# A recurrent attention and a three-way maxout layer on one core: another order for every engine's work and for both load queues

## Chip, core and metric

The kernel runs on 1 core of one Trainium2 chip. The metric is the device time of one launch, in microseconds (us), as the median of several runs. The engines that it uses are TensorE (PE: matrix products, with PEld for its weight loads), VectorE (DVE), ScalarE (ACT), GpSimd (POOL) and SyncE (SP, which only issues DMAs here).

## What is computed

```python
for t in range(S):                       # B, H, S, D = 4, 8, 768, 48
    state = alpha[:, :, t, :, None] * state + einsum('bhd,bhe->bhde', k[:, :, t], v[:, :, t])
    y[:, :, t] = einsum('bhd,bhde->bhe', q[:, :, t], state)
x = y.transpose(0, 2, 1, 3).reshape(B * S, H * D)      # 3072 x 384
h = maximum(maximum(x @ w1, x @ w2), x @ w3)           # 3072 x 768
out = h @ w_out                                        # 3072 x 384
```

Inputs and output are float32; q, k, v and alpha are 4 x 8 x 768 x 48, the weights 384 x 768 (three) and 768 x 384.

## The kernel before

The recurrence is done in chunks. There are 12 steps; step s is a window of 256 tokens of batch s % 4 (window s // 4), and has two units of 128 tokens (U = 2). A token row pair is folded into one partition (R = 2), so that a tile holds 128 partitions of 8 heads, 2 tokens and 48 numbers.

For each step the decays are logarithms that a triangular product sums (c, `sums`), and their exponentials scale q and k (`decay_in`, `decay_out`, `totals`, `scale_k`, `scale_q`). q and k are turned by PE (T and t) in steps 0 to 4 and by a transposing DMA (D) in steps 5 to 11. The scores (A) are masked on DVE (a), and the outputs are the chunk's own part and the state's part (Y, `attend`). The state is updated (S, s), decayed (M, z) and spread (y). Then x is kept in float16 (x), and the layer follows: nine gate pieces G per step, of six products each, with their maxima (h), and the output pieces O with a scaling and a store (o).

What runs when is written out by hand. `ORDER` is a string of some 800 pieces. A piece is a letter, a number, an optional engine (v, p or a for DVE, POOL or ACT) and `@step`. `emit` calls one function per piece, and every engine executes its pieces in the order of the string; waits between engines are put in by the framework (`tc.manual_schedule`). So the string is also the order of the two load queues:

- `l0`, `l1`, `l2`, `l3` load alpha, k, q and v of a step (384 KB each); without a letter they are issued by SP, with `a` by ACT, between ACT's own computing pieces. Each input has a ring of four tiles (`NQ`), so a load of step s waits for the readers of step s - 4.
- `K0` to `K8` load parts of w1, w2, w3 (`K` number i: weight i % 3, columns i // 3), `K9` to `K11` parts of w_out, into eight staging tiles; `W` casts the part to float16. `G`'s number is 3 x (pair of column tiles) + weight, so `G0` needs `W0`, `G1` needs `W1`, and so on.
- Stores (`o`) and transposing DMAs (`D`) are issued by SP, in the same queue as its loads.
- `H` is an idle product: `warm` multiplies a zero tile, 128 x 512, as often as its number says, and nothing reads the result.

All results of PE go to one pool of eight banks (`bank`); a new one waits until the last reader of the bank's previous content is done. An idle product takes a bank too, once per call.

```python
    queues = {"": nc.sync, "a": nc.scalar}
    def warm(_, n, *x):
        wps = bank([P, 512], "wps")
        for _ in range(n):
            nc.tensor.matmul(wps, blank[:, :P], blank, start=True, stop=True)
```

Of the kernel before, what the change touches and what calls it, by code (L numbers as in the profile page):

```python
# [23 lines left out]
def kernel(  # L24
# [422 lines left out]
    def emit(order):  # L447
# [20 lines left out]
        W7p@0 r0@5 G7@2 h7v@2 T0@3 q1p@3 T1@3 G7@1 z0p@3 K8@0 e0@4 w0p@4 f0@4 l3@4 s1v@3 v0a@3
        t1v@3 t0a@3 k1v@4 G6@0 h6a@1 q1p@4 h7v@1 l2@6 u0p@4 c0@5 A0@3 a0@3 A1@3 T1@4 q0p@4 a2@3
        W8a@0 G8@2 a3@3 h8v@2 G8@0 g0@5 h6a@0 a1@3 f0@5 G8@1 k0p@4 T0@4 e0@5 h8v@1 G7@0 v1p@3  # L470
        Y0@3 Y2@3 t1a@4 V0a@4 t0a@4 h7v@0 y0p@3 Y3@3 x0a@3 x1a@3 K11@0 l1@5 K9a@0 v1p@4 S0@4
        W11a@0 A0@4 s0v@4 K10a@0 a1@4 A1@4 a3@4 M0p@4 z0p@4 s1v@4 u0p@5 G0@3 l0@6 a0@4 G7@3
        l1a@6 a2@4 v0v@4 y0a@4 m0p@6 r0@6 G3@3 h3a@3 G1@3 G6@3 Y0@4 r1@5 l3a@5 h0v@3 Y3@4 h8v@0
        Y2@4 x1v@4 N0@6 Y1@4 x0a@4 W9a@0 l2@5 G8@3 M1v@1 c0@6 e0@6 f0@6 G0@4 h1v@3 k0v@5 q1v@5
        G3@4 w0v@5 q0v@5 M0p@5 W10a@0 g0@6 u0v@6 r1@6 G1@4 l0@7 m0v@7 G2@4 k1p@5 D1@5 h0a@4
        z1p@1 k0p@6 O0@1 h1v@4 w0v@6 D0@5 q0p@6 D0@6 k1p@6 q1p@6 O1@1 N0@7 l0@8 h6a@3 l3@6 h2v@4
        l2@7 l1a@7 o1a@1 h7v@3 D1@6 h3v@4 o0a@1 V0a@5 O0@2 o0a@2 O1@2 y1p@1 G7@4 h8v@3 S0@5 A0@5
# [6 lines left out]
        a0@6 Y2@6 Y0@6 O1@0 x1v@6 o0a@0 l0@10 r1@8 l3a@8 x0v@6 G4@6 G3@6 V0a@7 v1a@7 G0@6 h5v@5
        M1v@4 z1p@4 G8@5 h2v@5 h3a@6 h7v@5 h4v@6 S0@7 h0a@6 v0p@7 l3@11 o1a@0 h8v@5 y1a@4 A0@7
        a1@7 s0v@7 u0p@8 A1@7 a2@7 m0p@9 a3@7 M0p@7 z0p@7 y0p@7 k0p@8 Y1@7 a0@7 r0@9 l1a@9 G2@6
        G1@6 h1v@6 q1p@8 G6@6 h6v@6 s1v@7 G5@6 Y0@7 Y2@7 N0@9 l2@9 m0v@10 w0v@8 q0p@8 D0@8 Y3@7
        k1v@8 D1@8 x0a@7 x1a@7 l3@9 G8@6 G7@6 r1@9 G6@7 h6a@7 G0@7 V0v@8 c0@9 e0@9 O1@3 g0@9
        M1p@5 u0v@9 k0v@9 O0@3 f0@9 w0p@9 G4@7 q1p@9 k1p@9 D1@9 q0p@9 D0@9 o1a@3 o0a@3 V0a@11
        h2v@6 h5v@6 h7v@6 h8v@6 G8@7 G7@7 h7v@7 h0a@7 S0@8 N0@10 s0v@8 O0@5 o0a@5 A0@8 a0@8 A1@8  # L490
        a2@8 l0@11 Y1@8 G3@7 v1a@8 h3a@7 l1a@10 O1@5 c0@10 a3@8 z0p@8 y0p@8 Y3@8 o1a@5 a1@8 Y2@8
        e0@10 h8v@7 g0@10 v0p@8 Y0@8 G1@7 x0a@8 f0@10 V0a@9 v0p@9 x1v@8 G1@8 h4v@7 l2@10 M1v@6
        z1v@6 z1v@5 y1a@5 l3@10 G0@8 h1v@7 M0p@9 h0a@8 S0@9 A1@9 A0@9 s0v@9 z0p@9 y0p@9 G6@8
        l1@11 G2@8 a0@9 v1p@9 G2@7 G5@7 h6a@8 r0@10 r1@10 M0p@10 u0p@10 Y3@9 a3@9 a1@9 a2@9
        m0v@11 l2a@11 q1p@10 k1v@10 D1@10 Y0@9 Y1@9 x0a@9 Y2@9 G7@8 h2v@7 h1v@8 x1a@9 r0@11 G4@8
        G8@8 G6@9 G3@9 w0p@10 N0@11 c0@11 f0@11 h5v@7 e0@11 h6v@9 V0v@10 q0v@10 k0p@10 D0@10
        O0@4 O1@4 g0@11 v0a@10 h7v@8 h2v@8 G4@9 h8v@8 G5@8 O1@7 r1@11 v1p@10 S0@10 h3a@9 h4v@9
        o0a@4 o1a@4 q1p@11 k1v@11 o1a@7 M1p@7 D1@11 s0v@10 A0@10 a0@10 A1@10 a3@10 u0p@11 k0p@11
        G7@9 z0p@10 y0a@10 y1p@6 G8@9 G3@8 h3a@8 O0@7 a1@10 w0v@11 a2@10 h7v@9 h8v@9 Y3@10 Y1@10
        Y0@10 Y2@10 G1@9 G0@9 x1v@10 x0a@10 G4@10 z1p@7 q0p@11 D0@11 h4v@8 h0a@9 h5v@8 h1v@9  # L500
        G2@9 G3@10 o0a@7 v1p@11 h2v@9 S0@11 s0v@11 A0@11 A1@11 a0@11 a3@11 h3a@10 G6@10 G0@10
# [42 lines left out]
```

## Time and profile before

| | |
|---|---|
| median of 3 runs | 150.43 us (149.96 to 150.75) |
| profiled execution: span from first to last instruction | 147.1 us |
| the median less the span (launch and end, outside the span) | 3.3 us |
| PE / DVE / ACT / POOL busy | 137.7 / 120.5 / 100.7 / 89.7 us |
| idle products (L435) | 35, 9.7 us busy |
| loads and stores | 32.43 MB, 220 GB/s over the span |
| DMA issues of loads: SP / ACT | 50 / 10 |

The page's first part gives each engine's busy time. The second cuts the span into 40 slices of 3.7 us, with a busy digit for each. The chain of waits goes back from the last instruction to what released it. A timeline row reads: start, duration, engine, line, operation, output and inputs by the program's names, how many were merged, and in brackets the idle time before and what ended it. `SPq` and `ACTq` are the issuing of DMAs by an engine's sequencer. Names: `ra rk rq rv` are the loaded inputs, `ws` a staged weight, `wcat` a cast one, `lps` the sums, `aps` scores, `yps` outputs, `gps` gate products, `ops` output products, `wps` idle products, `ob` what is stored.

### The profile page before, as it was taken

Reading aid. Unit: us, or ns where it says so; the run is one execution under the profiler, and the core shown is the slowest. Engines: PE = TensorE matmul, PEld = TensorE weight load, DVE = VectorE, ACT = ScalarE, POOL = GpSimd, SP = SyncE. Lnnn points to the kernel's source line nnn. Section 1 sums busy time; section 2 is a strip of 40 time slices with the busy share of each in tenths; the row PEclk is TensorE's granted clock in tenths of the full one; section 3 lists DMA queues with packets and bytes.
Section 4 is the critical chain, followed back from the end, with each engine's and each line's share of the span. In section 5 each row is a group of like instructions: output and inputs, shape, how many; then the busy total and the mean of one; then the engine's idle time right before and its main releaser. Section 6 shows DMA issues by size and latency. Waiting matters only on the chain.

```text
span 147.1 us, 5524 instructions
## 1 busy us (share of the span) xinstructions
PE 137.7 (94%) x2301; PEld 105.4 (72%) x2301; DVE 120.5 (82%) x224; ACT 100.7 (68%) x207; POOL 89.7 (61%) x147
## 2 busy tenths in 40 slices
PE   6996888999999999999999999999899999999990
...
ACT  3669998878999978958699467795375463213170
...
DMA  5999999999999978999999979999987880021163
GB/s 114 321 325 341 326 312 282 322 288 334 328 298 241 286 225 155 202 289 187 303 156 325 327 218 155 237 269 276 288 117 222 91 113 0 4 75 37 53 241 134
DMA packets 73032, 32.43 MB, mean 220 GB/s; under 512 B 65456, under 2 KB 73008, under 8 KB 73008
## 3 DMA queue, kind: packets, MB, share of 16 engines
...
## 4 chain that ended last, share of the span: by engine, by line
PE 38%; DMA 18%; POOL 16%; ACT 9%; SPq 8%; issue 4%; DVE 4%; POOLq 0%; DVEq 0%; ACTq 0%
PE gps L388 21%; DMA rv<-in_v_dram 11%; PE ops L421 10%; SPq L96 7%; POOL qk L231 6%; DMA ws<-in_moe_w_dram 5%; PE yps L306 3%; DMA qkT<-qk 3%; POOL kept L372 2%; POOL ka L198 2%; PE aps L286 2%; POOL st L151 2%; ACT vu L149 1%; POOL wcat L151 1%; POOL vu L151 1%
## 5 line engine op out<-in xcount | busy, mean ns | idle before, releaser
L388 PE MATMUL gps<-xT,wcat 128*128 128x256 f16 x648 | 76.5, 273 | 1.5 <-DVE hT L405 0.6
L388 PEld LDWEIGHTS <-wcat 128*128 128x128 f16 x648 | 61.2, 98 | 11.7 <-issue 1.1
L293 DVE TENSOR_TENSOR lat<-aps,cp 128x512 f16<-128x512 f32 x48 | 30.3, 681 | 0.5 <-PE aps L286 0.3
L405 DVE TENSOR_TENSOR h<-gps,h 128x512 f16<-128x512 f32 x36 | 24.6, 684 | 2.4 <-PE gps L388 1.2
L405 DVE TENSOR_TENSOR hT<-gps,h 128x512 f16<-128x512 f32 x36 | 24.1, 684 | 1.9 <-PE ops L421 1.3
L421 PE MATMUL ops<-wo,hT 128*128 128x384 f16 (+1 forms) x150 | 25.2, 320 | 0.2 <-ACT h L149 0.2
L149 ACT CAST h<-gps 128x512 f16<-128x512 f32 x28 | 16.2, 583 | 9.0 <-PE gps L388 7.0
L421 PEld LDWEIGHTS <-hT 128*128 128x128 f16 x150 | 14.1, 98 | 8.2 <-issue 0.4
L155 ACT ACTIVATE ob<-ops,c 128x384 f32<-128x384 f32 (+1 forms) x23 | 12.2, 567 | 11.4 <-PE ops L421 11.3
L372 POOL TENSOR_TENSOR kept<-full,gm 128x192 f32<-128x192 f32 x18 | 10.3, 573 | 10.5 <-DVE gm L344 5.0
L151 POOL COPY vu<-vt 64x384 f16<-64x384 f16 x24 | 12.2, 509 | 4.7 <-ACT vt L155 2.8
L149 ACT CAST xT<-yps 128x384 f16<-128x384 f32 x17 | 7.8, 490 | 7.3 <-PE yps L306 7.3
L231 POOL TENSOR_TENSOR qk<-ka,ic 128x384 f16<-128x384 f32 x10 | 10.5, 1054 | 3.6 <-ACT h L149 2.6
L149 ACT COPY vu<-vt 64x384 f16<-64x384 f16 x22 | 11.2, 510 | 0.7 <-DVE vt L157 0.3
L435 PE MATMUL wps<-wo 128*128 128x512 f16 x35 | 9.7, 425 | 1.2 <-DVE wo L511 1.2
L155 ACT ACTIVATE vt<-rv,c 128x768 f16<-128x768 f32 x10 | 9.4, 941 | 1.6 <-DMA rv<-in_v_dram 1.5
L231 POOL TENSOR_TENSOR qk<-rq,ac 128x384 f16<-128x384 f32 x8 | 8.3, 1036 | 1.7 <-DMA rq<-in_q_dram 1.7
L286 PE MATMUL aps<-qkT 48*64 48x128 f16 x384 | 7.7, 219 | 1.3 <-DVE qkT L151 0.8
L198 POOL TENSOR_TENSOR ka<-rk,ra 128x384 f32<-128x384 f32 x8 | 8.4, 1044 | 0.2
L306 PE MATMUL yps<-lat,vu 128*32 128x128 f16 x384 | 8.0, 220 | 0.3 <-DVE lat L293 0.2
L231 POOL TENSOR_TENSOR qk<-rk,ic 128x384 f16<-128x384 f32 x6 | 6.2, 1040 | 3.1 <-DMA rk<-in_k_dram 3.0
L192 ACT ACTIVATE ra<-ra 128x384 f32<-128x384 f32 x12 | 6.3, 524 | 2.5 <-DMA ra<-in_alpha_dram 2.4
...
## 6 DMA issues: line engine op xcount, KB each, us to landing
...
```

The costliest lines, as they stand in the source:

```text
L149: nc.scalar.copy(out=dst, in_=src)
L151: engines[eng].tensor_copy(out=dst, in_=src)
L155: nc.scalar.mul(dst, src, col)
L198: engines[eng or "p"].tensor_mul(near_of[s, "k"], raw("k", s, 0), raw("a", s, 1))
L231: engines[eng or "p"].tensor_mul(dst.rearrange("p a b c -> p (a b) c")[:, :, :D], near_of.pop((s, n)) if r == 0 else raw(n, s, r), dec_of[ ...
L286: nc.tensor.matmul(aps[i][r * J:(r + 1) * J, a * U + x, :], qkT[rows, r, 1, p, cols], qkT[rows, :, 0, p, cols], start=True, stop=True)
L293: nc.vector.tensor_mul(lat_of[s, u][:, i], aps_of[s, u][i], pmask.unsqueeze(1).broadcast_to([P, HP, P]))
L306: nc.tensor.matmul(y_of[s, x][C * m:C * (m + 1), f, :], lhs, rhs, start=(s, x, m) not in begun, stop=last[x] and n == len(todo) - 1)
L372: engines[eng or "p"].tensor_mul(kept, full_of.pop((s, x)), gm_of.pop((s, x)).unsqueeze(2).broadcast_to([P, HP, D]))
L388: nc.tensor.matmul(gps[:, j, :], wcat[:, f, g, jj * P:(jj + 1) * P], xT[:, f].rearrange("p u t -> p (u t)"), start=(f == 0), stop=(f == NF ...
L405: nc.vector.tensor_max(h, gps, h_of[s, i - 1])
L421: nc.tensor.matmul(ops_of[s, o], hT_of[s][:, jj, u * P:(u + 1) * P], wo16[:, jj, cols], start=(jj == 0), stop=(jj == NJ - 1))
```

## The change

Only the string changes. The same pieces are in it, apart from the idle products: eight calls (12, 4, 1, 1, 4, 10, 1 and 2 products) become 35 calls of one product each, of which 16 stand ahead of the first sums (`c0@0`), 11 more ahead of the first `T`, and 8 later in the head. All else is in a new order on every engine. 22 loads are issued by ACT in place of 10, among them k and alpha of steps 0 to 2, `K2`, then `l2a@2 K5a K4a l0a@4` and `l2a@3 l2a@4` in the head. Some pieces change engine: the first `m` from POOL to DVE; four `z`, three `M`, three `o`, two `x`, one cast and one `t` more on DVE; four `V` on POOL in place of ACT (two) and DVE (two); three `v` from POOL to ACT and two `x` from ACT to DVE. The last pieces are a half row in place of a whole one.

The head, a stretch of the middle and the end of both strings:

```diff
@@ -451,59 +451,56 @@
 ...
     ORDER = """
-        l0@0 r0@0 H12@0 H4@0 H1@0 m0p@0 N0@0 c0@0 r1@0 l0@1 m0v@1 l2@0 H1@0 r0@1 f0@0 g0@0 H4@0
-        w0p@0 l1@0 u0v@0 q0v@0 N0@1 c0@1 e0@0 l3@0 V0a@0 r1@1 e0@1 f0@1 l0@2 k1v@0 q1v@0 M0p@0
-        l2@1 k0p@0 l1@1 k1p@1 m0v@2 w0v@1 H10@0 g0@1 N0@2 S0@0 s0a@0 T1@0 t1a@0 c0@2 q1v@1 T0@0
-        z0p@0 f0@2 e0@2 g0@2 q0v@1 H1@0 l3@1 V0a@1 t0v@0 A1@0 A0@0 T1@1 H2@0 u0v@1 a2@0 k0p@1
-        S0@1 T0@1 K1@0 v1a@0 v0p@0 a1@0 a3@0 a0@0 Y0@0 W1a@0 Y2@0 t1v@1 y0p@0 s0a@1 M0p@1 z0p@1
-        Y3@0 l0@3 v1a@1 t0v@1 m0v@3 A1@1 A0@1 x0a@0 x1a@0 G1@0 K2@0 W2p@0 G2@0 l1@2 a2@1 v0a@1
-        y0p@1 Y3@1 k1p@2 u0p@2 a1@1 N0@3 c0@3 a3@1 a0@1 Y0@1 r0@2 r1@2 K0@0 W0a@0 x0v@1 Y2@1
-        x1a@1 l2@2 s1v@0 s1v@1 f0@3 k0p@2 w0v@2 G0@0 l3@2 M0p@2 G1@1 G0@1 G2@1 h0a@0 q1v@2 T1@2
-        g0@3 K5@0 K3@0 e0@3 h1v@0 V0a@2 S0@2 s0a@2 h0v@1 q0p@2 h1v@1 T0@2 t0a@2 t1v@2 W5p@0 G5@1
-        G5@0 W3a@0 z0p@2 y0a@2 s1v@2 l0@4 v1p@2 h2v@0 K4@0 h2v@1 r0@4 A1@2 A0@2 a0@2 G3@1 h3a@1
-        Y3@2 m0p@4 W4p@0 l3a@3 a3@2 G3@0 N0@4 a1@2 v0p@2 l1@3 r0@3 G4@1 c0@4 g0@4 a2@2 Y2@2
-        x1v@2 h3a@0 Y0@2 x0a@2 u0p@3 h4v@1 l0@5 G4@0 h5v@1 M1p@0 z1p@0 y1a@0 G0@2 h0a@2 G5@2
-        r1@3 G1@2 K6@0 W6a@0 G3@2 h4v@0 h5v@0 h1v@2 G2@2 l2@3 k0p@3 w0v@3 q0v@3 K7@0 G6@2 V0a@3
-        h3a@2 l2@4 l1@4 r1@4 m0p@5 M0p@3 h2v@2 G4@2 h4v@2 k1p@3 S0@3 s0v@3 N0@5 G6@1 h6a@2 h5v@2
-...
-        s0v@5 o1a@2 a0@5 a1@5 A1@5 a3@5 a2@5 v1a@5 z0p@5 G4@4 v0p@5 r0@7 u0p@7 y0a@5 G2@3 G6@4
-        s1v@5 M1p@2 z1p@2 y1p@2 h4v@4 c0@7 Y3@5 Y1@5 Y2@5 m0p@8 Y0@5 e0@7 k0p@7 h2v@3 h6v@4
-        h7v@4 G5@4 x0a@5 f0@7 G4@3 x1a@5 l1@8 N0@8 G8@4 V0a@6 h8v@4 r1@7 w0p@7 G0@5 h0a@5 h5v@4
-...
-        G2@10 x0a@11 G8@10 x1a@11 G8@11 G5@10 h5v@9 G5@11 h6a@10 h0v@10 h1v@10 G0@11 h0v@11 O0@8
-        o0v@8 O1@8 o1a@8 h5v@10 G7@10 G3@11 h7v@10 h3a@11 G1@11 h8v@10 h2v@10 G2@11 h1v@11 G7@11
-        G6@11 h6a@11 G4@11 O1@9 h4v@11 O0@9 o0v@9 h2v@11 O0@6 O1@10 o1a@10 O1@6 h7v@11 h5v@11
-        O4@11 h8v@11 o1a@9 O6@11 o0a@6 o1a@6 o2a@11 O2@11 O3@11 o0a@11 O5@11 o1a@11 O0@10 o0a@10
+        l1a@0 l0@0 m0v@0 r0@0 N0@0 l0@1 l0a@2 l2@0 l3@0 l2@1 l1a@1 m0v@1 K2a@0 r0@1 r1@0 l3@1 l1@2 K0@0
+        H1@0 H1@0 H1@0 H1@0 H1@0 H1@0 H1@0 H1@0 H1@0 H1@0 H1@0 H1@0 H1@0 H1@0 H1@0 H1@0 c0@0 N0@1 f0@0
+        w0v@0 q0v@0 q1v@0 u0p@0 r1@1 e0@0 g0@0 H1@0 H1@0 H1@0 H1@0 c0@1 f0@1 g0@1 k1v@0 V0a@0 k0v@0 H1@0
+        H1@0 H1@0 H1@0 H1@0 H1@0 H1@0 T1@0 T0@0 m0v@2 t0v@0 w0v@1 v1a@0 q1v@1 N0@2 t1a@0 q0v@1 u0v@1 M0p@1
+        v0p@0 M0p@0 c0@2 H1@0 e0@1 k1p@1 k0p@1 H1@0 H1@0 S0@0 A0@0 A1@0 f0@2 g0@2 H1@0 H1@0 a0@0 a3@0 T1@1
+        H1@0 H1@0 T0@1 a1@0 a2@0 t1v@1 e0@2 s0a@0 V0a@1 t0v@1 z0p@0 y0p@0 W2p@0 u0p@2 K1@0 l2a@2 K5a@0
+        l0@3 K4a@0 l3@2 K3@0 l0a@4 l1@3 l3@3 Y2@0 Y0@0 Y3@0 H1@0 A0@1 S0@1 x0v@0 s1v@0 v0a@1 v1a@1 x1a@0
+        r0@2 s0a@1 W0a@0 l2a@3 K6@0 l2a@4 K7@0 W1a@0 A1@1 G2@0 G0@0 G1@0 a0@1 a2@1 a3@1 a1@1 m0v@3 r0@3
+        r1@2 N0@3 Y0@1 Y2@1 x0a@1 z0p@1 k1p@2 y0p@1 Y3@1 x1a@1 h0a@0 s1v@1 q1v@2 c0@3 w0v@2 k0v@2 h1v@0
+        h2v@0 T1@2 M0p@2 q0p@2 G2@1 G0@1 T0@2 G1@1 V0p@2 t0v@2 S0@2 e0@3 t1a@2 h0a@1 f0@3 g0@3 h1v@1 W5p@0
+        s0a@2 W3p@0 z0p@2 v1a@2 A0@2 A1@2 v0p@2 k1p@3 M0p@3 u0p@3 a1@2 a3@2 a2@2 a0@2 s1v@2 h2v@1 G5@0
+        G5@1 G3@1 G3@0 y0a@2 W4a@0 Y2@2 Y0@2 Y3@2 G4@0 m0v@4 h3a@0 r1@3 x0a@2 N0@4 h3a@1 V0a@3 r0@4 x1v@2
+        G4@1 h4v@0 h5v@0 h4v@1 q1v@3 h5v@1 G3@2 G0@2 c0@4 l1a@4 K8@0 k0p@3 K11a@0 l0@5 W6v@0 w0v@3 l0@6
+        l3@4 g0@4 v0a@3 h0a@2 S0@3 r1@4 s0a@3 l0@7 h3a@2 l1a@5 G1@2 f0@4 e0@4 K9@0 v1p@3 q0p@3 T1@3 G2@2
+        G4@2 G5@2 G6@1 T0@3 W7p@0 K10a@0 z0p@3 w0p@4 h1v@2 t1v@3 h4v@2 h5v@2 h2v@2 s1v@3 m0v@5 q0v@4 W8a@0
+        t0a@3 G7@1 G8@0 A1@3 A0@3 u0p@4 M0p@4 k0p@4 k1p@4 q1p@4 h6a@1 r0@5 y0a@3 N0@5 G6@2 G6@0 a3@3 a0@3
+        h7v@1 a1@3 r1@5 h6a@0 G7@0 a2@3 h7v@0 c0@5 G8@1 T0@4 G7@2 G8@2 T1@4 h8v@1 f0@5 e0@5 h6a@2 g0@5
+        h8v@0 h7v@2 t1v@4 V0a@4 t0a@4 Y0@3 Y2@3 Y3@3 x0a@3 x1a@3 S0@4 m0p@6 k1p@5 M1p@0 z1v@0 s0v@4 l2@5
+        l2a@6 l1@7 l3@5 l0a@8 M1p@1 W10p@0 m0p@7 z0p@4 W11a@0 y1a@0 N0@6 W9a@0 A1@4 A0@4 G6@3 G0@3 a0@4
+...
+        Y2@5 Y1@5 Y0@5 D0@6 r1@8 x1a@5 x0a@5 S0@6 A1@6 A0@6 a3@6 a1@6 s0v@6 z1v@3 a0@6 l2@8 l0a@9 l3@8
+        l1@8 v0a@6 V0a@7 M1p@4 z0p@6 y0p@6 u0p@8 m0p@9 D0@7 l0a@11 D1@7 l3@9 l0a@10 l2@11 l1@9 l2@9 l3@11
+...
+        Y2@10 Y0@10 Y3@10 x1v@10 S0@11 A1@11 A0@11 x0a@10 a3@11 a2@11 a1@11 s0v@11 a0@11 h8v@9 z0v@11 O0@8
+        G0@10 y0a@11 G4@10 G1@10 G2@10 G4@9 Y1@11 Y0@11 h0v@10 o0v@8 h1v@10 Y3@11 Y2@11 x0v@11 x1v@11
+        G6@10 h2v@10 h4v@9 G3@10 h3a@10 h6a@10 G1@11 G5@10 G8@10 h4v@10 G7@10 G0@11 G7@11 G5@9 O1@8 h5v@10
+        h7v@10 h5v@9 h8v@10 h0v@11 O0@9 G6@11 h1v@11 O0@10 o0a@10 G2@11 O1@10 G3@11 h2v@11 h6v@11 h3a@11
+        o1a@10 o1a@8 o0a@9 G4@11 G5@11 G8@11 h7v@11 h4v@11 h5v@11 h8v@11 O1@9 O2@11 O3@11 O4@11 O5@11
+        o1a@9 o0a@11 o1a@11 O6@11 o2a@11
```

More of the change, by code (lines that the diff above doesn't have):

```diff
@@ L466 @@
-        r1@3 G1@2 K6@0 W6a@0 G3@2 h4v@0 h5v@0 h1v@2 G2@2 l2@3 k0p@3 w0v@3 q0v@3 K7@0 G6@2 V0a@3
-        h3a@2 l2@4 l1@4 r1@4 m0p@5 M0p@3 h2v@2 G4@2 h4v@2 k1p@3 S0@3 s0v@3 N0@5 G6@1 h6a@2 h5v@2
[L468 to L477, printed above, removed]
@@ L478 @@
-        s0v@5 o1a@2 a0@5 a1@5 A1@5 a3@5 a2@5 v1a@5 z0p@5 G4@4 v0p@5 r0@7 u0p@7 y0a@5 G2@3 G6@4
-        s1v@5 M1p@2 z1p@2 y1p@2 h4v@4 c0@7 Y3@5 Y1@5 Y2@5 m0p@8 Y0@5 e0@7 k0p@7 h2v@3 h6v@4
-        h7v@4 G5@4 x0a@5 f0@7 G4@3 x1a@5 l1@8 N0@8 G8@4 V0a@6 h8v@4 r1@7 w0p@7 G0@5 h0a@5 h5v@4
-        h4v@3 k1v@7 G3@5 h3a@5 G1@5 h1v@5 c0@8 e0@8 g0@7 f0@8 M1p@3 G5@3 h5v@3 G4@5 Y1@6 A1@6
-        g0@8 M0p@8 r0@8 h4v@5 A0@6 a1@6 l3@7 S0@6 s0v@6 M0p@6 q0v@7 D0@7 q1p@7 z0p@6 D1@7 G6@5
-        a3@6 h6a@5 G7@5 l0@9 l2@8 G5@5 G2@5 z1p@3 O0@0 s1v@6 v1a@6 a2@6 y0a@6 y1p@3 v0a@6 Y3@6
@@ L484 @@
[L484 to L501, printed above, removed]
@@ L502 @@
-        M0p@11 z0p@11 G5@9 G1@10 y0v@11 a1@11 y1a@7 Y1@11 Y3@11 v0a@11 a2@11 Y0@11 Y2@11 h4v@10
-        G2@10 x0a@11 G8@10 x1a@11 G8@11 G5@10 h5v@9 G5@11 h6a@10 h0v@10 h1v@10 G0@11 h0v@11 O0@8
-        o0v@8 O1@8 o1a@8 h5v@10 G7@10 G3@11 h7v@10 h3a@11 G1@11 h8v@10 h2v@10 G2@11 h1v@11 G7@11
-        G6@11 h6a@11 G4@11 O1@9 h4v@11 O0@9 o0v@9 h2v@11 O0@6 O1@10 o1a@10 O1@6 h7v@11 h5v@11
-        O4@11 h8v@11 o1a@9 O6@11 o0a@6 o1a@6 o2a@11 O2@11 O3@11 o0a@11 O5@11 o1a@11 O0@10 o0a@10
+        l1a@0 l0@0 m0v@0 r0@0 N0@0 l0@1 l0a@2 l2@0 l3@0 l2@1 l1a@1 m0v@1 K2a@0 r0@1 r1@0 l3@1 l1@2 K0@0
@@ new lines @@
+        h7v@1 a1@3 r1@5 h6a@0 G7@0 a2@3 h7v@0 c0@5 G8@1 T0@4 G7@2 G8@2 T1@4 h8v@1 f0@5 e0@5 h6a@2 g0@5
+        h8v@0 h7v@2 t1v@4 V0a@4 t0a@4 Y0@3 Y2@3 Y3@3 x0a@3 x1a@3 S0@4 m0p@6 k1p@5 M1p@0 z1v@0 s0v@4 l2@5
+        l2a@6 l1@7 l3@5 l0a@8 M1p@1 W10p@0 m0p@7 z0p@4 W11a@0 y1a@0 N0@6 W9a@0 A1@4 A0@4 G6@3 G0@3 a0@4
+        h8v@2 a2@4 G7@3 G1@3 w0p@5 v0p@4 h0v@3 a1@4 q1v@5 a3@4 h6a@3 r0@6 y0a@4 u0v@5 v1a@4 V0a@5 q0v@5
+        O1@1 l1@6 D1@5 l3a@7 k0p@5 c0@6 O1@2 O0@2 O0@1 s1v@4 h1v@3 h7v@3 D0@5 Y2@4 Y0@4 Y1@4 Y3@4 g0@6
@@ new lines @@
+        e0@6 N0@7 r1@6 f0@6 x1a@4 x0v@4 z1v@1 l2@7 l3@6 G3@3 G8@3 G0@4 o1v@1 h8v@3 h0v@4 M0v@5 c0@7 G2@3
+        G1@4 G2@4 r0@7 o0a@1 o0v@2 o1a@2 h3a@3 g0@7 y1a@1 e0@7 f0@7 h1v@4 h2v@3 A1@5 S0@5 A0@5 G3@4 s0v@5
+        a0@5 a3@5 M1p@2 u0p@7 a1@5 a2@5 h2v@4 w0p@6 q0p@6 k1p@6 q1p@6 m0p@8 u0p@6 k0p@6 k0p@7 z0p@5 D1@6
+        v1a@5 N0@8 h3a@4 r1@7 M1p@3 z1p@2 y0p@5 q1p@7 w0p@7 k1p@7 G4@4 c0@8 G5@4 G4@3 q0p@7 G6@4 G5@3
+        h4v@3 h4v@4 M0v@6 G8@4 G7@4 g0@8 e0@8 r0@8 v0a@5 V0a@6 f0@8 h6a@4 s1v@5 h5v@3 h5v@4 h7v@4 Y3@5
@@ new lines @@
+        Y2@5 Y1@5 Y0@5 D0@6 r1@8 x1a@5 x0a@5 S0@6 A1@6 A0@6 a3@6 a1@6 s0v@6 z1v@3 a0@6 l2@8 l0a@9 l3@8
+        l1@8 v0a@6 V0a@7 M1p@4 z0p@6 y0p@6 u0p@8 m0p@9 D0@7 l0a@11 D1@7 l3@9 l0a@10 l2@11 l1@9 l2@9 l3@11
+        O0@0 G6@5 s1v@6 h6a@5 G7@5 w0v@8 y1a@2 v1a@6 G0@5 O1@0 G2@5 G1@5 k1v@8 h7v@5 o1a@0 h0a@5 a2@6
+        h8v@4 o0v@0 h1v@5 N0@9 G3@5 Y0@6 Y1@6 Y2@6 Y3@6 G4@5 h3a@5 x0a@6 x1a@6 c0@9 M0p@7 h2v@5 q1v@8 G5@5
+        G3@6 G4@6 h4v@5 h5v@5 g0@9 h3a@6 f0@9 e0@9 h4v@6 G8@5 S0@7 h8v@5 k0p@8 V0p@8 v1p@7 q0p@8 D0@8
```

13 lines of the change are left out of this document (added).

## The prediction

> **What bounds the kernel now.** I read the page first: busy shares, slices, data rate.
>
> ```profile
> PE 137.7 (94%) x2301; PEld 105.4 (72%) x2301; DVE 120.5 (82%) x224; ACT 100.7 (68%) x207; POOL 89.7 (61%) x147
> PE   6996888999999999999999999999899999999990
> ACT  3669998878999978958699467795375463213170
> DMA  5999999999999978999999979999987880021163
> GB/s 114 321 325 341 326 312 282 322 288 334 328 298 241 286 225 155 202 289 187 303 156 325 327 218 155 237 269 276 288 117 222 91 113 0 4 75 37 53 241 134
> ```
>
> TensorE (PE) is the bound, except in the first 25 us, where its digits are 6 to 8 while ScalarE (ACT) and DMA stand at 8 and 9. A busy PE is not a PE at its peak, so I take the price of a product from stretches without a wait, in the chain of waits:
>
> ```profile
> 123.83 0.90 PE yps L306 x56
> 124.73 4.04 PE gps L388 x36
> 128.77 1.95 PE ops L421 x12
> 143.21 0.58 ACT ob L155
> ```
>
> That is 0.112 us a gate product (0.68 for a piece G of six), 0.163 an output product (0.97 for a full O), 0.90 for the four Y of a step. By the same view A costs 0.26, T 0.46, S 0.37 (0.19 in the last four steps), c 0.24. Over the program: G 108 x 0.68 = 73.4; O 23.3; A 6.2; Y 9.9; T 4.6; S 3.7; c 2.9; in all 124.0 us of work, without the idle products. The span of 147.1 has 23.1 us more. Where they lie is seen in the timeline of PE:
>
> ```profile
> 1.19 5.15 PE L435 MATMUL wps<-wo 128*128 128x512 f16 x17 [1.19 <-DVE wo L511]
> 22.52 2.79 PE L388 MATMUL gps<-xT,wcat 128*128 128x256 f16 x24 [0.56 <-ACT wcat L149]
> ```
>
> At 22.52 `G0@0` starts, released by the cast of a weight on ACT (`W0a@0`). Ahead of it in the order stand 7.3 us of the 124.0, so PE is 22.52 - 7.3 = 15.2 us behind: the **head**. The last product ends at 143.1, 19.1 behind: the **middle** loses 3.9 more. The **tail** to the span's end takes 4.0 (scaling, store, end). 124.0 + 15.2 + 3.9 + 4.0 = 147.1.
>
> Now what the loads do to the queue that issues them. SP's timeline, ACT's timeline, and the chain of waits:
>
> ```profile
> 3.24 1.20 SPq L96 DMA_DIRECT2D rk<-in_k_dram  x1
> 4.49 1.15 SPq L96 DMA_DIRECT2D rv<-in_v_dram  x1
> 5.68 1.15 SPq L96 DMA_DIRECT2D ra<-in_alpha_dram  x1
> 13.97 3.09 SPq L107 DMA_DIRECT2D ws<-in_moe_w_dram  x1
> ...
> 4.42 0.52 ACT L192 ACTIVATE ra<-ra 128x384 f32<-128x384 f32 x1 [2.41 <-DMA ra<-in_alpha_dram]
> 29.40 0.42 ACTq L96 DMA_DIRECT2D rv<-in_v_dram  x1
> ...
> 29.40 6.54 DMA rv<-in_v_dram
> ```
>
> An issue on SP is not a fixed price. `l1@0` ends at 4.44, when the first alpha has just landed (ACT starts on it at 4.42); `l3@0` ends at 5.64, as the second lands (VectorE, DVE, starts on it at 5.72). So a queue takes about three loads of rows that have not landed, or four with weights among them, and then its issue stands until room is made. On SP that costs nothing, since SP computes nothing. ACT's ten issues took 0.37 to 0.49 each: it never had more than four in flight, two of them of w_out.
>
> **The change part by part.** Span and launch first: the profiled execution spans 147.1, the median of the runs is 150.43; I add 3.3 to a span.
>
> *Idle products*: 35 before, 35 after. The first 17 took 5.15 us; 16 end near 6.2, when `c0@0` can start anyway. The other 19 lie where PE waits for loads; two of them and `T0@1` may wait for a mask's bank, 0 to 0.5 us, hidden behind `k0p@1`. Cost 0; were that cover gone, 19 x 0.22 = 4 us at most, which no row suggests.
>
> *First sums*: k of step 0 goes on ACT's queue beside alpha, so alpha lands some 0.7 us later (a load is 0.39 MB, 1.21 us at the 325 GB/s of the second and third slices, and twice that when two queues share). `m0` on DVE (0.56) in place of GpSimd, POOL (0.99) gives back 0.43. `c0@0` starts near 6.4 against 6.18. Behind it `T1@0` waits for q and k, and these land no earlier and no later than before, as the rate is full. Cost 0 to 0.7, taken as 0, since the loads hide it.
>
> *More issues on ACT*: 22 against 10, at 0.42. In the trace of before an issue runs while ACT executes the piece ahead of it (29.40 lies inside an ACT row), so alone it is free.
>
> *Six loads on ACT in the head*: this is the term. ACT's new order reads `V0a@1 l2a@2 K5a@0 K4a@0 l0a@4 v0a@1 v1a@1 x1a@0 r0@2 s0a@1 W0a@0 l2a@3 l2a@4 W1a@0`. `V0a@1` waits for v of step 1, the tenth load: 2.5 + 10 x 1.21 + 0.4 to land = 15.0. Four issues at 0.42 from there put 16.8 on the clock, and ACT's queue is as full as SP's was when it stood. SP's queue is full at the same time (`K1 l0@3 l3@2 K3 ...`), so a load of ACT's takes 2.4 us. ACT reaches `l2a@4` at 16.8 + 1.05 + 1.05 + 0.38 + 0.43 + 0.27 + 0.73 + some 0.4 of waiting = 21.1, and asks for a sixth load. It gets room when q2, K5, K4 and a quarter of a4 have moved: 3.27 loads x 2.42 = 7.9 us after the data start at 16.8, so 24.7. Early bound 22.2 (hardly any wait: the queue takes one load more); late bound 26.7, by the last row shown, where one load of ACT's took 6.54 us from issue to landing beside SP's backlog. I take 24.7, between. Behind the waiting issue on ACT stand `W1a@0` (0.85), `r0@3`, `r1@2`, `N0@3`, `x0a@1`; PE waits for the first of them: `G1@0` needs it, and everything behind `G1@0` on PE. It starts at 25.55, and ahead of it stand 6.4 us of work (three c, four T, two S, four A, three Y, two G): 19.1 behind in place of 15.2. Price 3.9, bounds 1.2 to 5.9.
>
> *SP's queue*: with six loads fewer in the head it gets through `K0` as the twelfth load of all (17.0 + 0.4) and `K1` at half rate by 20.1, both ahead of their casts, so neither sets the time. Later `l2@8 l3@8 l1@8` stand behind `D0@6`, which waits for the scaled q and k of step 6; `w0v@8` and `u0p@8` follow within 3 us of PE work. If they are late, DVE and POOL wait 2 to 4 us, with `S0@8`, the first product of PE that needs them, 9 us of its work away: 0 for PE, and in the middle's range below.
>
> *The rest of the order*: the sums of rows per engine, each piece from its start to the next one's, hardly move: DVE 110.1 to 113.2, ACT 94.7 to 92.9, POOL 84.0 to 85.6 (its four `V0p` are not in the trace; between 0.82, POOL's 128x768 cast, and 2.0, two of its 384-wide products; I take 1.9, nearer the latter as they scale f32). All stay below PE. The old middle lost 3.9 us to late pieces; a new order has its own, and PE, 3.9 us later, gives loads and DVE more lead. From 1.0 to 4.5; I take 2.6, the midpoint.
>
> *Tail*: `O6` and `o2a` end it: a half row (0.43 and a 96 KB store) instead of a whole one (0.58, 192 KB), but two scalings follow each other. 0; kept at 4.1.
>
> Sum: 124.0 + 19.1 + 2.6 + 4.1 = 149.8 span, 153.1 us. Own range of this case 151.2 to 155.5, from the bounds of the stall and the middle.
>
> **The rivals.** *ACT is not held* (not slower): its queue takes six loads, as issues of 0.42 beside ACT's work. For it: no ACT issue of before took over 0.49. Against it: SP's rows, and that ACT never had so many in flight. It decides at the sixth load. Then `W1a@0` ends near 22.2, `G1@0` is 15.8 behind, and with 2.0 for the middle the span is 145.9, the time 149.2 (148.0 to 150.6). The Trainium skill, "DMA: Bandwidth & Descriptors", section "Issuing engines are not separate DMA queues", stands on this side for the issue: loads from several engines run on the same 16 DMA engines and interleave, and issuing from several only saves the sequencer's time, which it calls usually small. By that rule this rival's 149.2 would be the time; the trace agrees on the shared rate, but 3.09 us for one SP issue is not small.
>
> *The clock falls too*: PE stands at `G1@0` for about 3 us. In the weight loads of the idle products, starts were 0.43 us apart until 3.72 and 0.21 after, that is 2.5 us of half speed at the start though the granted clock reads 9 throughout. If the wait brings this back, 2.5 x 0.5 = 1.3 us, and with the late bound 155.6 (154.5 to 157). Nothing in before shows it: PE's longest idle time in the head after its start is 0.85 us. The Trainium skill, "TensorE: Matmul & The Clock Gate", section "HAM oscillation — how this bites in real kernels", asks for no PE gap over some 3.4 us; no run here shows that yet.
>
> *ACT is simply late*: no stall, but more of ACT's work is put ahead. When PE has done 35 us, the new order has placed 43.5 us of ACT's work, the old one 40.0. In 30 to 50 us ACT is busy 18.4 of 20, so 1.6 of these 3.5 fit: 1.9 later, 152.3 (151.3 to 153.2). Against it: some of it, `W9a@0` to `r0@6`, is not needed at once.
>
> **How the numbers follow.** ACT held 0.48, 153.1; not held 0.30, 149.2; clock too 0.10, 155.6; ACT late 0.12, 152.3. A measurement tells 0.5% (0.75 us). Below 149.7 lies seven tenths of "not held" and a trace of the forecast: 0.22. Within 0.5%: 0.11. Above 151.2: 0.67. The range runs from 148.6, which takes in most of "not held", to 155.8.
>
> **What would show it.** Right: ACT's issue of `l2a@4` takes 2 us or more, the weight cast behind it ends at 25 to 26, and `G1@0` starts at 25 to 26 with an idle time of over 2 us released by ACT's weight cast; the last product is 21 to 23 us behind 124.0. Wrong: all ACT issues at or under 0.5 us and a first steady gate stage by 22.5; or a middle that loses under 1 us, or over 5, with its own late load or piece.

## The result, and the profile after

| | before | after |
|---|---|---|
| median (lowest to highest) | 150.59 us (149.96 to 151.12) | 161.38 us (160.83 to 162.21) |
| span of the profiled execution | 147.1 us | 160.1 us |
| PE work without idle products | 124.0 us | 124.0 us |
| end of the last product, less that work | 19.1 us | 32.5 us |

The changed kernel takes 1.0734 times as long (95% interval 1.0666 to 1.0802). The forecast was 153.1, with a range to 155.8: the sign came out as forecast, the size did not. The profiled execution of after took 162.21, 2.1 us above its span. It is the longest of four, so the spans are 13.0 us apart where the medians are 10.8. In e2, e8, e10 and e11 below the profiled execution was a slow one of its kernel, so only places and waits are read from it.

The first two parts of the page of after:

```profile
PE 141.6 (88%) x2301; PEld 108.2 (68%) x2301; DVE 123.7 (77%) x234; ACT 97.6 (61%) x207; POOL 92.2 (58%) x137
PE   7929782399999997999999998999999999999991
ACT  3269780577997968997975818985653443120262
PEclk9995999659999999999999999999999999999998
GB/s 124 323 325 342 348 341 327 348 330 181 17 328 333 308 20 216 170 171 288 147 312 209 276 243 277 174 257 208 190 150 111 141 115 53 11 42 0 51 151 146
```

ACT is busy for less time than before (97.6 against 100.7), yet it has two holes, a 2 in the second slice and a 0 in the seventh (a slice is 4 us). PE has its own just behind, a 2 in the third and a 2 and a 3 in the seventh and eighth, and behind each the granted clock reads 5 or 6. Before, it was a steady 9:

```profile
PEclk9999999999999999999999999999999999999999
```

The data rate is full from the second to the ninth slice: the loads are not slower in sum, they hold the wrong engine.

ACT's timeline shows what stands in the holes. `ACTq` rows are ACT's own issues, between its computing rows:

```profile
5.68 0.60 ACTq L96 DMA_DIRECT2D rk<-in_k_dram  x1
6.32 3.11 ACTq L107 DMA_DIRECT2D ws<-in_moe_w_dram  x1
9.48 0.52 ACT L192 ACTIVATE ra<-ra 128x384 f32<-128x384 f32 x1 [3.70 <-issue]
...
17.83 0.53 ACTq L107 DMA_DIRECT2D ws<-in_moe_w_dram  x1
19.05 0.37 ACTq L96 DMA_DIRECT2D ra<-in_alpha_dram  x1
...
23.26 0.83 ACT L149 CAST wcat<-ws 128x768 f16<-128x768 f32 x1
25.94 0.37 ACTq L96 DMA_DIRECT2D rq<-in_q_dram  x1
29.42 0.37 ACTq L96 DMA_DIRECT2D rq<-in_q_dram  x1
29.83 0.83 ACT L149 CAST wcat<-ws 128x768 f16<-128x768 f32 x1 [5.74 <-DMA rk<-in_k_dram]
```

The first hold is one issue, `K2a@0`, that lasts 3.11 us: the fourth load that ACT has in flight (k0, a2 and k1 are ahead of it). SP's issues beside it stand too (2.36, 0.98 and 2.65 us for those that start at 4.67, 7.24 and 8.27). `r0@1`, and with it the sums of step 1, stand behind it. The second hold looks different: `l2a@3` and `l2a@4` take 0.37 us each, but start at 25.94 and 29.42, though ACT had been done since 24.1. The issues in the trace tell why. A semaphore is a counter that a load raises when it has landed; here the loads of both queues share eight of them, and a load waits until the load that had its semaphore before has landed. For `l2a@3` that is `K5a@0`, which landed 0.02 us before the issue began; for `l2a@4` it is `l1@3`, k of step 3, a load that SP issued at 18.85 and that landed 10.5 us later, again 0.02 us before the issue. So the trace names a load of k as the releaser of a weight cast that doesn't read k. ACT's own queue was not full: at 25.94 two of its loads were still in flight (`K4a@0`, `l0a@4`), and at 29.42 two again (`l0a@4`, `l2a@3`). SP, which computes nothing, loses no computing to the same kind of wait; on ACT the cast `W1a@0` stands behind it.

PE's timeline carries both holds on. The first row is of before (`c0@1`), the others of after:

```profile
7.85 0.32 PE L207 MATMUL lps<-la,cp 128*128 128x384 f16 x1 [0.17 <-ACT la L187]
...
10.88 0.32 PE L207 MATMUL lps<-la,cp 128*128 128x384 f16 x1 [3.03 <-ACT la L187]
13.35 1.91 PE L265 MATMUL tps<-cp,qk 128*128 128x128 f16 x16
...
24.15 0.83 PE L388 MATMUL gps<-xT,wcat 128*128 128x256 f16 x6 [0.16 <-ACT wcat L149]
30.72 1.46 PE L388 MATMUL gps<-xT,wcat 128*128 128x256 f16 x6 [5.74 <-ACT wcat L149]
```

`c0@1` starts at 10.9 instead of 7.8, `G1@0` at 30.7, 24.3 us behind the 6.4 us of work ahead of it. The six products of `G1@0` take 1.46 us where a piece of six takes 0.83 elsewhere: the clock had fallen in the wait. By the time that PE has done 10 us of work it is 26.7 us behind, against 15.1 before. From there to the last product after loses 5.8 us more, before 4.0.

### The profile page after: what moved, and what is told of

It is laid out like the page before. It is cut to its first block, busy times and chain, and to the rows that moved or that the text cites. A ratio compares the mean times of both kernels' runs of the same rounds, so it can differ in the third digit from the quotient of the medians.

```text
span 160.1 us, 5508 instructions
## 1 busy us (share of the span) xinstructions
PE 141.6 (88%) x2301; PEld 108.2 (68%) x2301; DVE 123.7 (77%) x234; ACT 97.6 (61%) x207; POOL 92.2 (58%) x137
## 3 DMA queue, kind: packets, MB, share of 16 engines
q10 hardware_dynamic: 19712, 8.75, 19.8%
## 4 chain that ended last, share of the span: by engine, by line
PE 34%; DMA 21%; SPq 14%; POOL 12%; ACT 6%; DVE 6%; issue 3%; ACTq 1%; POOLq 0%; DVEq 0%
PE gps L388 18%; DMA rk<-in_k_dram 10%; PE ops L421 10%; SPq L96 7%; POOL qk L231 6%; DMA ws<-in_moe_w_out_dram 4%; SPq L107 4%; SPq L273 3%; PE yps L306 3%; DMA rq<-in_q_dram 3%; DMA out_dram<-ob 2%; DVE h L405 2%; DMA qkT<-qk 2%; POOL qa L202 2%; PE aps L286 1%
## 5 line engine op out<-in xcount | busy, mean ns | idle before, releaser
L388 PE MATMUL gps<-xT,wcat 128*128 128x256 f16 x648 | 78.7, 275 | 6.3 <-ACT wcat L149 6.1
L405 DVE TENSOR_TENSOR h<-gps,h 128x512 f16<-128x512 f32 x36 | 24.3, 682 | 4.5 <-ACT h L149 3.2
L155 ACT ACTIVATE ob<-ops,c 128x384 f32<-128x384 f32 (+1 forms) x20 | 10.9, 565 | 10.4 <-PE ops L421 10.3
L149 ACT COPY vu<-vt 64x384 f16<-64x384 f16 x28 | 14.2, 508 | 2.2 <-DMA ws<-in_moe_w_dram 1.1
L435 PE MATMUL wps<-wo 128*128 128x512 f16 x35 | 11.5, 470 | 2.3 <-DVE wo L508 1.2
L231 POOL TENSOR_TENSOR qk<-qa,ac 128x384 f16<-128x384 f32 x8 | 8.6, 1078 | 8.1 <-DVE qa L202 7.8
L202 DVE TENSOR_TENSOR qa<-rq,ra 128x384 f32<-128x384 f32 x7 | 3.9, 554 | 11.4 <-ACT ra L194 11.4
L151 POOL COPY vu<-vt 64x384 f16<-64x384 f16 x18 | 9.5, 526 | 5.0 <-issue 4.1
L231 POOL TENSOR_TENSOR qk<-rk,ic 128x384 f16<-128x384 f32 x10 | 10.3, 1029 | 1.7 <-ACT ic L217 1.6
L372 POOL TENSOR_TENSOR kept<-full,gm 128x192 f32<-128x192 f32 x14 | 7.3, 522 | 6.7 <-DVE full L367 4.2
L149 ACT CAST st<-kept 64x192 f16<-64x192 f32 x22 | 7.6, 347 | 3.9 <-DVE kept L372 3.7
L231 POOL TENSOR_TENSOR qk<-ka,ic 128x384 f16<-128x384 f32 x7 | 7.6, 1098 | 3.2 <-DVE ka L198 3.0
```

Source lines behind the costliest of these rows:

```text
L149: nc.scalar.copy(out=dst, in_=src)
L151: engines[eng].tensor_copy(out=dst, in_=src)
L155: nc.scalar.mul(dst, src, col)
L231: engines[eng or "p"].tensor_mul(dst.rearrange("p a b c -> p (a b) c")[:, :, :D], near_of.pop((s, n)) if r == 0 else raw(n, s, r), dec_of[ ...
L388: nc.tensor.matmul(gps[:, j, :], wcat[:, f, g, jj * P:(jj + 1) * P], xT[:, f].rearrange("p u t -> p (u t)"), start=(f == 0), stop=(f == NF ...
L405: nc.vector.tensor_max(h, gps, h_of[s, i - 1])
```

## The experiments

Each time stands with its ratio to the kernel before, measured beside it on the same chip, and the ratio's 95% interval. The kernel before itself ranged from 148.2 to 152.7 us in these sessions, and the runs were on several chips, so steps of the time of 1 us or less are not told apart. "Behind" is PE's start of a piece less the work ahead of it, by the prices of the prediction. The kernels e1 to e6 are after with some loads given back to SP, their places in the order kept.

**e1: the first hold alone.**

```
- K2a@0
+ K2@0
```

> The new kernel with one letter taken away: K2 is issued by SP at the same place of the string. Theory A (ACT is held by its own issues): ACT's hold of 3.1 us at 6.3 goes, the second sums start near 7.8 in place of 10.9, and PE is some 3 us earlier up to 24 us. But the second hold (the issue of l2a@4) ends when a load lands, and the loads run at full rate either way, so the third gate piece still starts at 29 to 31: the time falls by 0 to 2 us, to 159.5 to 161.4. Theory B (the new order is late for its own data, whoever issues): no change, and no earlier second sums. Theory C (each hold counts in full, they add up): 157.5 to 158.5.

Measured 159.13 us, ratio 1.061 (1.0522 to 1.0698). The first hold is gone, `c0@1` starts at 7.7; `G1@0` starts at 28.7, still behind a wait of ACT:

```profile
27.38 0.44 ACTq L96 DMA_DIRECT2D rq<-in_q_dram  x1
27.86 0.83 ACT L149 CAST wcat<-ws 128x768 f16<-128x768 f32 x1 [5.03 <-DMA rk<-in_k_dram]
```

The 3.2 us gained at `c0@1` are 2.0 at `G1@0` and 2.3 in the time, between theories A and C, and the interval overlaps that of after.

**e2: the second hold alone.**

```
- l2a@3  l2a@4
+ l2@3   l2@4
```

> The new kernel with q of steps 3 and 4 issued by SP in place of ACT, at the same places of the string. Theory A: ACT's wait of 5.7 us ahead of the cast W1 goes, G1 of step 0 starts at 24.5 to 25.5 in place of 30.7, PE's clock does not fall there, and the time is 5 to 7.5 us lower, 154 to 156.5. Theory B (order late for its data): G1 still waits for a weight or an input, 160 to 162.

Measured 158.36, ratio 1.0532 (1.0436 to 1.0628). `G1@0` starts at 25.0 instead of 30.7, which is the whole 5.7; but the time falls by 3.0 only, less than expected. Between 20 and 26 us of PE's work a new loss has come up, from 19.8 to about 25 behind: ACT now gets early to the next load that has to wait, `K10a@0`. The next run shows the same.

**e3: both.** The two edits above together.

> The new kernel with K2 and q of steps 3 and 4 issued by SP. Theory A: both holds are gone; G1 of step 0 starts at 22 to 23.5, behind by 16 to 17 us as before the change; the middle still loses 5 to 6.5 us, so 151 to 153.5. Theory B: 160 to 162. Theory C (holds add up in full, with no other limit behind them): 151 to 152.

Measured 156.16, ratio 1.0434 (1.034 to 1.0529), 2.7 us over the upper end of what was expected. `G1@0` starts at 23.7. PE is 17.8 behind until it has done 20 us of work, then 22.4 at 26. Here is the wait that shows itself once the other two are gone, on ACT and on PE:

```profile
43.10 0.38 ACTq L110 DMA_DIRECT2D ws<-in_moe_w_out_dram  x1
43.52 0.83 ACT L149 CAST wcat<-ws 128x768 f16<-128x768 f32 x1 [3.56 <-DMA rv<-in_v_dram]
```

```profile
40.71 0.82 PE L388 MATMUL gps<-xT,wcat 128*128 128x256 f16 x6
44.41 1.46 PE L388 MATMUL gps<-xT,wcat 128*128 128x256 f16 x6 [2.88 <-ACT wcat L149]
```

The load is `K10a@0`, the cast behind it `W8a@0`, the load waited for v of step 4. In e3 ACT's queue was not full there: from 41.6 on only one of its loads, `l1a@5`, was still in flight. In after, where everything is later, the same wait is 0.91 us on ACT and costs PE 0.18.

**e8: is it the shared semaphore that makes ACT wait?** e3 with two of SP's loads moved behind `K10a@0` in the order, so that `K10a@0` takes over another load's semaphore, that of `K9@0`. ACT's own pieces are untouched.

```
- l3@4 ... l0@7 ... K10a@0
+ K10a@0 l3@4 l0@7
```

> The third run's kernel (156.16 us), in which ACT idles 3.6 us ahead of the cast W8, with two loads of SP (v of step 4, alpha of step 7) moved behind K10 in the string; ACT's own issues stay what and where they are. Theory L (ACT's issue of K10 waits until the load that last used its completion counter has landed; the counters go round over both queues, and that load was v4, now it is K9): the idle time ends at the landing of K9, 1 to 2 us earlier, and the time falls by 0.5 to 2 us, to 154.2 to 155.7. Theory Q (ACT's own queue has no room): the idle time stays 3.6 us and ends at the same place, 155.7 to 156.7.

Measured 155.62, ratio 1.0403 (1.031 to 1.0497). The same wait of the same cast is now ended by the load whose semaphore was taken over:

```profile
43.77 0.37 ACTq L110 DMA_DIRECT2D ws<-in_moe_w_out_dram  x1
44.19 0.83 ACT L149 CAST wcat<-ws 128x768 f16<-128x768 f32 x1 [3.38 <-DMA ws<-in_moe_w_out_dram]
```

`K9@0` landed at 43.70 and the issue began at 43.77; v of step 4, which had ended the wait in e3, landed at 45.87 and no longer mattered. So the order of SP's loads decides what ACT waits for. The expected gain did not come: the wait hardly moved, 3.38 against 3.56, as `K9@0` landed no earlier than v of step 4 had, and the time is not told apart from that of e3.

**e4: all ten loads of the head on SP**, alpha ahead of k in the first two.

```
- l1a@0 l0@0   l0a@2 l1a@1 K2a@0 l2a@2 K5a@0 K4a@0 l0a@4 l2a@3 l2a@4
+ l0@0 l1@0    l0@2  l1@1  K2@0  l2@2  K5@0  K4@0  l0@4  l2@3  l2@4
```

> The new kernel with all ten loads of the head that ACT issued (k0, a2, k1, K2, q2, K5, K4, a4, q3, q4) issued by SP, at their places of the string; alpha of step 0 goes ahead of k of step 0. Theory A: as the run before it, or up to 1 us better, as no issue stands between ACT's pieces in the head: 150.5 to 153. If SP alone were too slow a queue for the loads of this order, the later loads (v1, K0, K1) would land later and the time would be over 154.

Measured 152.97, ratio 1.0177 (1.0094 to 1.0259). In its profile the clock is 1.000 again. PE is 17.9 behind at 15 to 20 us of work, 19.4 at 26: ACT still waits 1.79 us for `K10a@0`.

**e5: four more, to the 14th load.**

```
- l1a@4 K11a@0 l1a@5 K10a@0
+ l1@4  K11@0  l1@5  K10@0
```

> The fourth run's kernel (head loads on SP, 152.97 us) with the next four loads on ACT (k4, K11, k5, K10) also issued by SP. Theory A (ACT is held by its own issues): ACT's wait of 1.8 us ahead of the cast W8 goes, PE no longer loses 1.5 us between 20 and 26 us of its work, and the time is 151 to 152. Theory B (what is left is the order of the computing pieces): no change, 152.5 to 153.5.

Measured 152.10, ratio 1.017 (1.0082 to 1.0258). PE stays 17.9 behind at 26 us of work; the last product is 21.5 behind in its profile. The ratio is not told apart from that of e4. Against after, these 14 loads are the main cause: ratio 1.0734 comes down to 1.0170, three quarters of the loss, while the rest of the new order is kept.

**e6: all 22 on SP.** The eight loads that were left, `l2a@6` to `l1a@11`, go to SP too.

> All 22 loads that ACT issued are issued by SP, at their places of the string; nothing else. Theory A: each later hold (1.4 and 1.7 us at the loads of a8 and v7) goes too, so 150 to 151.5. Theory D: SP stands at the transposing DMAs of steps 5 to 11, and loads that ACT issued past them come later, so the middle loses more: 153 to 157. Theory B: as the run before it within 0.5 us.

Measured 159.76, ratio 1.0711 (1.0607 to 1.0815): theory D in kind, and more than it expected. SP's queue is not free everywhere. At 91 us of work PE is 21.6 behind (20.9 in e5), at 95 it is 30.6 behind. Two rows of the waits, engine and what it waited for, total, times and longest:

```profile
POOL qk L231 <- DMA rk<-in_k_dram: 7.0, 1, 7.0
PE yps L306 <- POOL st L151: 5.7, 1, 5.7
```

Late in the program SP carries transposing DMAs, which wait for scaled q and k, and the last loads of k stand behind them. There ACT was the right place: of these eight issues seven took 0.37 or 0.38 us in after, the other (`l0a@8`) 1.45.

**e7: the holds on the old order.** Before, with the same ten loads of the head issued by ACT.

```
- l1@0  l0@2  l1@1  K2@0  l2@2  K5@0  l0@4  K4@0  l2@3  l2@4
+ l1a@0 l0a@2 l1a@1 K2a@0 l2a@2 K5a@0 l0a@4 K4a@0 l2a@3 l2a@4
```

> The kernel before, with one part of the change alone: the same ten loads of the head (k0, a2, k1, K2, q2, K5, K4, a4, q3, q4) are issued by ACT, at their places in the old string; order, engines and idle products are as before. Theory A (issues on ACT hold ACT): the time rises by 2 to 8 us, to 152 to 158, with ACT idle in front of a piece for over 1 us, ended by the landing of a load or by an issue. Theory B (the new order is at fault): within 1 us of 150.0.

Measured 170.75, ratio 1.1405 (1.1284 to 1.1525): worse than after, and far over what either theory expected. PE is 20.4 behind at 5 us of work and 38.4 at 35, then loses as little as before. It is not the same way, though: in the old order ACT reaches the loads late, the first k is issued at 7.62 us, PE's clock falls three times, and DVE and POOL wait for data:

```profile
DVE ka L198 <- DMA rk<-in_k_dram: 7.3, 1, 7.3
POOL wcat L151 <- DMA ws<-in_moe_w_dram: 6.6, 2, 4.9
```

So the letters alone, without the new order, do more harm than both together; the new order had put the first of those issues early in ACT's list.

**e9: what the fallen clock costs by itself.** After, with 22 idle products in PE's wait ahead of `G1@0`.

```
- G2@0 G0@0 G1@0
+ G2@0 G0@0 H22@0 G1@0
```

> The kernel after with 22 idle products on PE ahead of G1@0, in the 5.7 us in which PE waits there for the weight cast. They take about 5 us, so G1@0 still starts near 30.7. Theory C (PE's lower clock after a wait costs time by itself): the six gate products of G1@0 take 0.83 us instead of 1.46, the products behind them run at full clock too, PEclk shows no 5 or 6 in the slices behind 30 us, and the kernel takes 1 to 1.5 us less than after, 160.0 to 160.4. Rival N (the lower clock falls in time in which PE would wait for ACT's catching up anyway): the products are shorter by the same amount, the waits behind them longer, and the time stays at 161.4, within 0.4.

Measured 160.22, ratio 1.0647 (1.0585 to 1.0709), 1.2 us under the median of after, though the intervals overlap. In PE's timeline the effect is plain:

```profile
25.50 5.74 PE L435 MATMUL wps<-wo 128*128 128x512 f16 x22
31.08 0.82 PE L388 MATMUL gps<-xT,wcat 128*128 128x256 f16 x6
...
33.28 1.47 PE L388 MATMUL gps<-xT,wcat 128*128 128x256 f16 x12
```

`G1@0` starts 0.4 us later than in after and takes 0.82 instead of 1.46; twelve more gate products take 1.47 instead of 2.05 (in after at 34.66). When 10 us of work are done, PE is 24.7 behind instead of 26.7. The wait itself is about as long (ACT's 5.52 for k of step 3), so these 2.0 us are the clock alone. The clock fell here too, but earlier: it reads 0.5 from 23.8 to 27.2 us, where PE's wait just ahead was 1.74, and the twelve gate products ahead of the idle ones take 2.44 us instead of 1.66.

**e10: the 16 idle products ahead of the first sums.** e5 without them.

```
- H1@0 (16 times) c0@0
+ c0@0
```

> The kernel with 14 loads moved to SP's queue (152.1 us, span 149.0), without the 16 idle products ahead of the first sums. Theory of the prediction (they lie in time in which PE waits for its first input, and cost nothing): c0@0 stays at 6.3 within 0.1, and leaving them out brings no gain; what they may bring is the clock: without them the first 30 us show a lower granted clock in some slices, and the kernel takes 0 to 1 us more, 152.1 to 153.1. Rival P (they delay the first sums): c0@0 starts 0.2 us or more earlier, everything behind it too, and the time falls to 151.9 or less.

Measured 153.54, ratio 1.0188 (1.0118 to 1.0259) against e5's 1.017: not told apart (the medians, 1.4 us apart, are from two chips). `c0@0` starts at 5.7 instead of 6.3, so the products do delay the first sums, by 0.6 us, as the rival had it; but `T1@0` starts at 11.4 in place of 11.3, and PE's lag is the same to 0.1 us up to 50 us of work. The loads hide those 0.6 us, and the time did not fall. PEclk reads 9 in every slice of the head, yet the first products run slowly: the first sums take 0.48 us instead of 0.33, the next four idle products 1.87 instead of 1.02, the seven that start at 8.81 2.73 instead of 1.67. From 11 us on the products are as short as in e5. So the 16 do bring the clock up; the page doesn't show it, as the clock's record in this trace begins at 11.0 us only; here that is worth nothing, since `T1@0` waits for its data anyway.

**e11: the end of the order alone.** Before, with the last output piece moved ahead of step 11's.

```
- O4@11 h8v@11 ... O5@11 o1a@11 O0@10 o0a@10
+ O0@10 o0a@10 O4@11 h8v@11 ... O5@11 o1a@11
```

> The kernel before with only the end of its order changed: the last output products O0@10 and their copy stand ahead of O4@11, so that the last thing written is step 11's half row. In the changed kernel the stretch from the last product to the end of the span is 3.6 us against 4.0. Theory T (the tail's shorter end comes from the order of the last stores): 0.3 to 0.5 us less than before, 149.6 to 149.9, ratio 0.997. Rival U (the last store's fixed time decides, whichever row it is): no change, ratio 1.000 within 0.001.

Measured 151.18, ratio 1.0076 (1.003 to 1.0122). Both theories missed: it is slower. In its profile 4.9 us pass from the last product to the end of the span, before 4.0, after 3.6; ACT's last two scalings now end a wait for a store:

```profile
146.17 0.92 ACT L155 ACTIVATE ob<-ops,c 128x384 f32<-128x384 f32 x2 [0.31 <-DMA out_dram<-ob]
```

That accounts for 0.3 of it; what makes up the rest is open. This profile can't price the tail: its last product is already 21.5 behind, against 19.1 before, and 1.6 of these 2.4 us are there at 26 us of work, far ahead of the edit.

**e12: one late load of the head.** e5 with alpha of step 3 three loads earlier in SP's queue.

```
- K1@0 l2@2 K5@0 l0@3
+ l0@3 K1@0 l2@2 K5@0
```

> The kernel with 14 loads moved to SP's queue (152.1 us, span 149.0), and with the load of step 3's alpha three loads earlier in SP's queue, ahead of the weights K1. There DVE and ACT waited 0.63 and 1.03 us for that load, and PE 0.82 us for ACT's gate of step 3 at 25.1 us, behind. Theory A (what is left of the loss in the head, 17.9 us behind against 15.5 before at 26 us of work, is in part this late load): c0@3 starts near 24.3, the offset at 26 us of work is 17.2 or less, and the kernel takes 0.5 to 0.8 us less, 151.3 to 151.6. Rival B (the loss was made earlier, by 22 us, in the order of the pieces, and the weights delayed by the moved load take the gain back): offset at 26 us of work 17.7 to 18.2, time 152.1 within 0.3.

Measured 151.54, ratio 1.0139 (1.0098 to 1.0179) against 1.017. At 26 us of work PE is 17.3 behind instead of 17.9, and `T1@2`, which follows the sums of step 3, starts at 24.1 instead of 25.4; but at the end it is 21.6 behind, as far as in e5. The gain in the head is there, and in this profile it was given back later. The time moved by half a microsecond in the expected direction, inside both intervals: undecided. No version tried here beats the kernel before.

## Why the prediction was right and wrong, point by point

*Six loads on ACT in the head* was the right term with the wrong size, and in part the wrong cause. The forecast had one hold at `l2a@4`, from a full queue, an issue of 2 us or more, `W1a@0` done at 25.55 and `G1@0` 19.1 behind (bounds 1.2 to 5.9 for the price of 3.9). `G1@0` started 24.3 behind, a price of 9.1. The engine, the load, the cast behind it and the product that waits are as forecast. The step that failed is its price: two waits of ACT that the sum did not have, in place of one wait for room. In detail:

- A hold earlier on was not priced at all. The forecast said that a queue takes three loads of rows, or four with weights among them, and applied it to ACT only from `V0a@1` on. The same rule on `l1a@0 l0a@2 l1a@1 K2a@0` would have raised the question; the issue of `K2a@0` took 3.11, and e1 gives 2.0 us of it at `G1@0`.
- The second hold is not an issue that stands for room: both issues took 0.37. It is a wait ahead of the issue, for landings (25.94 and 29.42), and it is 5.74 us long on ACT and on PE. e2 removes exactly this from `G1@0`'s start, and e8 shows in a like place that the other load's landing is what counts. Room was there: two of ACT's loads were in flight, where the forecast's rule allows three or four. The cost of a load on a computing engine is thus set by another load, here one of SP's that took 10.5 us to land behind SP's backlog.
- The rest is neither: 1.4 us by these two prices (9.1 less 2.0 and 5.7), 2.1 by e3, which with both holds gone starts `G1@0` 17.3 behind, against the 15.2 of the head before. That part lies with the order and the remaining issues; e4, with all ten on SP, starts `G1@0` 16.2 behind, so each has about half of it.

*The clock falls too*, a rival at 0.10 and 1.3 us, was true as a mechanism and added to the forecast instead of standing beside it: 1.46 in place of 0.83 for `G1@0`, and 2.0 us in all by e9. Behind `G1@0` the head went from 24.3 to 26.7 behind. (With the late bound, the rival's own terms add up to 156.4, where it wrote 155.6.) The Trainium skill, "TensorE: Matmul & The Clock Gate", section "HAM oscillation — how this bites in real kernels", puts the fall at PE gaps of more than about 3.4 us. The 5.74 us gap agrees; in e3 a gap of 2.88 us already did the same (1.46), so here the measured row is stricter than the page. In e1 the clock fell at 18.5 us with no gap over 1.09 ahead of it, so these runs show no gap length that is safe.

*ACT is not held* (0.30, 149.2) is refuted by both holds. On its side the prediction had weighed the Trainium skill, "DMA: Bandwidth & Descriptors", section "Issuing engines are not separate DMA queues", by which issuing from several engines only saves sequencer time that is usually small. The shared rate agrees again (323 to 348 GB/s from the second to the ninth slice of after); the small sequencer time does not, with 3.11 us for one issue on an engine that had computing to do. *ACT simply late* can't be seen beside the holds: ACT has fewer busy microseconds than before.

*More issues on ACT, alone free* was half right: 0.37 or 0.38 for seven of the eight late ones, and e6 shows the loss when they are taken away; but not in the head.

*Idle products 0* and *first sums 0 to 0.7, taken as 0* were right in price. `c0@0` started at 6.6 against the 6.4 forecast. But the 16 products don't end before `c0@0` could start, as was said: e10 shows 0.6 us of delay, which the loads hide.

*SP's queue* cost PE nothing that the waits of after show. e6 shows how near the limit is: eight loads more, behind the transposing DMAs, cost 9 us of PE's time.

*The middle* was put at 2.6 (1.0 to 4.5); it lost 5.8, over the upper bound. The largest single idle times of PE behind 40 us are 0.76, 0.76 and 0.39; behind the first, `O1@1`, an issue `l0a@8` of 1.45 us stands ahead of a cast on ACT. From 15 us of work to the last product after loses 5.8 us, e5 without the earlier holds 3.6, and before 3.6 as well. So the forecast's lead for loads and DVE brought nothing, and about 2.2 us come with the issues that e5 gives back; which of them, no run shows.

*`V0p` on POOL* was put at 1.9 between 0.82 and 2.0; it takes 2.20, over the upper bound:

```profile
88.51 2.20 POOL L157 TENSOR_SCALAR vt<-rv,c 128x768 f16<-128x768 f32 x1
```

*The tail* was put at 4.1 and is 3.6. *Span to time*: the 3.3 us added to a span set a median beside the span of a quick execution. One execution of after takes about 2.1 us more than its own span (162.21 and 160.1), so this term was 1.2 too large and hid as much of the miss.

The sum: 124.0 + 26.7 + 5.8 + 3.6 = 160.1 for the span. Against the forecast's 149.8 that is 7.6 more in the head (5.2 up to `G1@0`, 2.4 behind it while the clock was low), 3.2 in the middle, 0.5 less in the tail. The range given for its main case was also narrower than its own terms: the bounds of the stall and the middle together give 148.8 to 157.0, not 151.2 to 155.5, and the early bound 22.2 gives a price of 1.4, not 1.2. Even 157.0 would not have held the result. What stays open is the share that is neither one of these 14 loads nor the clock: e5's ratio of 1.017, some 2.5 us, of which e12's late alpha is perhaps half a microsecond.
